# Moving whole rounds of a short convolution from TensorE to VectorE in a fused convolution and multiplicative FFN

## The chip, the cores and the metric

The kernel runs on one core of a Trainium2 chip. The metric is device time in microseconds, and less is better. The time before is the median of 3 runs; a profile shows one further execution.

## The reference

The input `x` has 8 sequences of 3904 tokens with 192 channels. First a causal convolution of 7 taps runs along each sequence. The taps are a softmax over each of 8 heads' weights, and a head has 24 channels. Then a feed-forward network without a nonlinearity other than a product is applied to each token:

```python
# attention-like part: w = softmax(weight, axis=-1), one row of 7 taps for each head of 24 channels
out[b, s, h, g] = sum_k w[h, k] * x_pad[b, s + k, h, g]      # x_pad: 6 zero rows ahead of each sequence
# feed-forward part, on the 31232 tokens
a = x @ w1            # 192 -> 1024
b = x @ w2            # 192 -> 1024
h = a * b @ w3        # (a * b) @ w3, 1024 -> 1024
return h @ w_out      # 1024 -> 192
```

The kernel multiplies `w3 @ w_out` once at its head (`W_sb`, 1024 x 192), so a token needs two first products and one second product.

## The kernel before, in words

The 31232 tokens are two streams of 15616 (`NS = 2`, four sequences each), worked on side by side: stream 0 on partitions 0 to 63 and stream 1 on partitions 64 to 127. The 192 channels are three groups of 64 (`k` = 0, 1, 2). A round `R` is 512 tokens of each stream; there are 31 rounds (`NR`), the last with 256 tokens.

**First product** (`first_product`, L455 to L468): for each of 8 slices of 128 of the hidden width, TensorE multiplies the weights by `xT[k]` (channels on partitions, tokens along the free dimension) into two PSUM tiles `pa` and `pb`. ScalarE copies `pa` to `asb` (L462), VectorE multiplies `asb` by `pb` into `abT` (L464). `xT` is a ring of 4 rounds.

**Second product** (`second_product`, L480 to L488): 32 matmuls of `abT` by `W_sb` for one round and stream, one copy by ScalarE to `osb`, one output DMA on SyncE's queue.

**Convolution on TensorE** (`conv`, L294): tokens are cut into windows of 32 rows that give 26 outputs (`ST`), with the 6 rows ahead. Windows are loaded by GpSimd's DMAs, which cast to bf16, into tiles `xb` (`load_x`, L127), and multiplied by 32x32 band matrices `Aband`, one for each head. The results are evicted to `convo` (L303). Windows are grouped into blocks: `SIZES = [20, 20, 20, 40] + [64] * 7 + [56]`. A *unit* is one call of `conv` for some channels of a block. When all units of a block are done, `store` (L329, L335) writes it to the DRAM array `rows` from SyncE's queue, and `transposes` (L369) brings it back as `xT` by transposing DMAs, also from SyncE's queue. The window in which a new sequence starts needs zero rows ahead of it: GpSimd memsets them in `xb` (L629). From block 4 on (`SPLIT`) the blocks carry two of the three channel groups (`WC = 128`).

**Convolution on VectorE**: the third group, from round 5 on. `cast_c` (L394) casts its channels to a DRAM array `rows_c` from GpSimd's queue, `raw_transpose` (L400) brings two rounds back as `raw`, channels on partitions, and `conv_c` (L410, L414) applies the 7 taps as one multiplication and six multiply-adds with the tap as a scalar of each partition (`wC`), into `xT[2]`. The taps reach `wC` through DRAM (`load_taps`, L377 and L383).

**Order.** The order of instructions on each engine is the order in which the program records them; engines wait for each other by semaphores. After a head, which does rounds 0 to 2, the blocks 0 to 3 and `W_sb`, the loop at L626 goes through phases. Phase p records the first products of rounds 2p+1 and 2p+2 (phase 0 has none), then `conv_c`, then four second products of the rounds 2p and 2p+1, with conv units after the first and, in some phases, after the third (`places`). The transposes are recorded at the end of a phase, and the rounds that they bring are used in the phase after the next:

```python
        if p < len(chunks):
            raw_transpose(p)
        while sent[0] < NR and sent[0] <= LAG + 2 * p + 4 and \
                min((sent[0] + 1) * CH, TS) <= stored[0]:
            transposes(sent[0])
            sent[0] += 1
```

In the head, `load_taps`, `cast_c(0)` and the load of block 5 are recorded in `later_loads`, inside round 0.

Of the kernel before, what the change touches and what calls it, by code (L numbers as in the profile page):

```python
# [11 lines left out]
ALU = mybir.AluOpType  # L12
# [4 lines left out]
def kernel(  # L17
# [29 lines left out]
    WB = -(-S // ST)  # L47
    NWIN = (B // NS) * WB
    LAST = S - (WB - 1) * ST
    LAG_ROWS = (LAG + 1) * CH  # L50
    SIZES = [20, 20, 20, 40] + [64] * 7 + [56]
    SPLIT = 4
    WC = 2 * Q
    assert sum(SIZES) == NWIN
    NB = len(SIZES)
    FIRST = [sum(SIZES[:b]) for b in range(NB)]
    RC = FIRST[SPLIT] * ST // CH
    XN = 32 * WC
    HW = 6

    def tok(i):
        return (i // WB) * S + (i % WB) * ST

# [17 lines left out]
    rows_c = dram.tile([TS, NS * Q], BF16, name="rows_c")  # L81
# [9 lines left out]
    def width_of(b):  # L91
        return D if b < SPLIT else WC

    def parts_of(b):
        return [range(4)] if 4 * shape_of(b)[1] * width_of(b) <= XN else [range(2), range(2, 4)]
# [6 lines left out]
    def runs_of(b, js, e):  # L102
        n, m, E = shape_of(b)
        runs = []
        for s, i in enumerate(FIRST[b] + j * n + u * E + e for j in js for u in range(m)):
            if i < HW or i == NWIN - 1:
                continue
            if runs and tok(i) == runs[-1][1] + runs[-1][2] * E * ST:
                runs[-1][2] += 1
            else:  # L110
                runs.append([s, tok(i), 1])
        return runs

    def load_x(b, parts=(0, 1)):
# [3 lines left out]
        for js in [v for q, v in enumerate(parts_of(b)) if q in parts]:  # L118
            wd = width_of(b)
            xb = work.tile([128, XN], BF16, tag="xb", bufs=6, name="xb")  # L120
            xb = xb[:, 0:len(js) * m * wd].rearrange("p (w d) -> p w d", d=wd)
            for j in js:
                tiles[j] = (xb, (j - js[0]) * m)
            for e in range(E):
                for s, t, w in runs_of(b, js, e):
                    for r in range(NS):
# [3 lines left out]
                                        ap=[[D, C], [E * ST * D, w], [1, wd]]))  # L130
                for j in js:
                    for u in range(m):
                        i, s = FIRST[b] + j * n + u * E + e, tiles[j][1] + u
                        if i % WB == 0 and i:
                            zeros_of += [(xb, group(r, e).start, s) for r in range(NS)]
                        if i == NWIN - 1:
                            nc.gpsimd.memset(xb[group(1, e), s, :], 0.0)
                            t = tok(i) - PAD
                            nc.gpsimd.dma_start(out=xb[group(0, e), s, :],
                                                in_=x_rows[t:t + C, 0:wd])  # L140
                            p = group(1, e).start
                            nc.gpsimd.dma_start(out=xb[p:p + PAD + LAST, s, :],
                                                in_=x_rows[TS + t:TS + t + PAD + LAST, 0:wd])
# [132 lines left out]
    def conv(b, c0, wd, evict=(nc.scalar.copy,), es=None):  # L276
        n, m, E = shape_of(b)
        es = range(E) if es is None else es
        if b not in convo_of:
            convo_of[b] = work.tile([128, n, width_of(b) // Q, NS, Q], BF16, tag="convo", bufs=2,  # L280
                                    name="convo")
            left_of[b] = width_of(b) * E
# [27 lines left out]
    stored, sent = [0], [3]  # L310

    def store(b, first=0):
        stored[0] = tok(FIRST[b] + SIZES[b]) if b + 1 < NB else TS
        n = SIZES[b] // 4
        convo = convo_of[b]
        cols = slice(0, NS * width_of(b))
        for j in range(4):
            w = 0
            while w < n:
                i = FIRST[b] + j * n + w  # L320
                if i < first:
                    w += 1
                    continue
                left = WB - 1 - i % WB
                src = convo[C * j:C * j + ST, w:w + max(1, min(n - w, left))]
                src = src.rearrange("s w k r g -> s w (k r g)")
                j0 = tok(i)
                if left == 0:
                    nc.sync.dma_start(out=rows[j0:j0 + LAST, cols], in_=src[0:LAST, 0, :])  # L329
                    w += 1  # L330
                    continue
                m = min(n - w, left)
                dst = rows[j0:j0 + ST * m, cols].rearrange("(w s) c -> s w c", s=ST)
                for s0, s1 in ((0, 16), (16, ST)):
                    nc.sync.dma_start(out=dst[s0:s1], in_=src[s0:s1])  # L335
# [29 lines left out]
    def transposes(R, first=0):  # L365
        t0, t1 = max(R * CH, first), min((R + 1) * CH, TS)
        a = t0 % RING
        for k in range(NP if R < RC else WC // Q):
# [5 lines left out]
    wC = const.tile([128, K], FP32)  # L374

    def load_taps():
        nc.sync.dma_start(out=taps_d, in_=taps)  # L377
        for r in range(NS):
            c = WC
            while c < D:  # L380
                h = c // G
                c1 = min(h * G + G, D)
                nc.sync.dma_start(out=wC[r * Q + c - WC:r * Q + c1 - WC, :],  # L383
                                  in_=taps_d[h:h + 1, :].to_broadcast([c1 - c, K]))
                c = c1

    chunks = [(R * CH, min((R + 2) * CH, TS)) for R in range(RC, NR, 2)]
    raw_of = {}

    def cast_c(i):  # L390
        t0, t1 = chunks[i]
        t0 = t0 if i else t0 - HALO
        for r in range(NS):
            nc.gpsimd.dma_start(out=rows_c[t0:t1, r * Q:r * Q + Q],  # L394
                                in_=x_rows[r * TS + t0:r * TS + t1, WC:D])

    def raw_transpose(i):
        t0, t1 = chunks[i]
        raw_of[i] = work.tile([128, HALO + 2 * CH], BF16, tag="raw", bufs=2, name="raw")
        nc.sync.dma_start_transpose(out=raw_of[i][:, 0:HALO + t1 - t0],  # L400
                                    in_=rows_c[t0 - HALO:t1, :])

    def conv_c(i):
        t0, t1 = chunks[i]
        raw = raw_of.pop(i)
        acc = work.tile([128, 2 * CH], FP32, tag="acc", bufs=1, name="acc")
        starts = [z for z in range(0, TS, S) if t0 <= z < t1]

        def times(out, lo, hi, d):
            nc.vector.tensor_scalar(out=out, in0=raw[:, HALO + lo - t0 - d:HALO + hi - t0 - d],  # L410
                scalar1=wC[:, K - 1 - d:K - d], scalar2=None, op0=ALU.mult)

        def add(out, lo, hi, d):
            nc.vector.scalar_tensor_tensor(  # L414
                out=out, in0=raw[:, HALO + lo - t0 - d:HALO + hi - t0 - d],
                scalar=wC[:, K - 1 - d:K - d], in1=acc[:, lo - t0:hi - t0],
                op0=ALU.mult, op1=ALU.add)

        times(acc[:, 0:t1 - t0], t0, t1, 1)
        for z in starts:  # L420
            nc.vector.memset(acc[:, z - t0:z - t0 + 1], 0.0)
# [3 lines left out]
        for lo in range(t0, t1, CH):  # L425
            hi = min(lo + CH, t1)
            add(xT[2][:, lo % RING:lo % RING + hi - lo], lo, hi, 0)
# [11 lines left out]
    def first_product(R, between=None):  # L439
# [3 lines left out]
        r0 = (R * CH) % RING  # L443
        per = CH // N if CH % N == 0 else 1
        for f0 in range(0, JT, per):
            pq = []
            for i in range(2):
                p = banks("pa" if i == 0 else "pb")
                pq.append(p)
                for f in range(per):  # L450
                    ft = f0 + f
                    for k in range(NP):
                        for r in range(NS):
# [4 lines left out]
                                xT[k][rs, r0:r0 + N],  # L458
# [15 lines left out]
    def second_product(R, r):  # L474
# [3 lines left out]
        for g in range(ng):  # L478
# [8 lines left out]
        t0 = r * TS + R * CH  # L487
        nc.sync.dma_start(  # L488
            out=out[t0:t0 + ng * 128, :].rearrange("(g p) d -> p g d", p=128), in_=osb)
# [3 lines left out]
    def last_product(R, r):  # L493
        ab = abT_of.pop(R)
        for g, f in zip(range(width(R) // 128), (nc.scalar.copy, nc.vector.tensor_copy) * 2):
# [84 lines left out]
    def later_loads():  # L580
# [6 lines left out]
        load_taps()  # L587
        cast_c(0)
        load_x(5)
# [17 lines left out]
               (store, 3), (transposes, 3), (transposes, 4))})  # L607
    sent[0] = 5
# [4 lines left out]
    units = [(b, c) for b in range(SPLIT, NB) for c in range(0, WC, Q)]  # L613
    loads = [(b, e) for b in range(6, NB) for e in range(len(parts_of(b)))]

    def convolve():
        b, c = units.pop(0)
        conv(b, c, Q, (A, A))
        if c + Q == WC:
            store(b)  # L620

    places = {0: 2, 1: 2, 2: 1, 3: 1, 4: 2, 5: 1, 6: 1, 7: 1, 8: 1, 9: 2, 10: 1, 11: 1}
# [62 lines left out]
```

## Time and profile before

| | |
|---|---|
| median of 3 runs | 520.54 us (519.78 to 521.62) |
| the profiled execution | 517.63 us |
| span in its profile, first to last instruction | 515.9 us |
| TensorE matmuls busy | 510.2 us, 6271 instructions |
| VectorE busy | 423.2 us |
| ScalarE busy | 339.0 us |
| GpSimd busy | 82.9 us |
| first products (L455), all matmuls | 2976 |
| second products (L480) | 1936 matmuls |
| convolution on TensorE (L294) | 1216 matmuls, 222 ns each in the median, many at once |
| convolution on VectorE (L410, L414) | 13 + 106 instructions, 110.7 us |
| DMA, moved | 60.76 MB |

How to read it: PE is TensorE, DVE VectorE, ACT ScalarE, POOL GpSimd and SP SyncE; a `q` behind the name is the engine's queue of instructions that issue DMAs or wait. Matmuls on different parts of TensorE's array overlap, so their durations do not add up to busy time. A timeline row gives start, duration from the first to the last of the instructions that it merges, engine, line, operation, what it writes and reads, and a count. Rows by stretch of time give the stretch, its length, busy microseconds of PE, PEld (weight loads), DVE, ACT and POOL with counts, the granted clock of TensorE, the busy microseconds of a mean DMA engine, and GB/s.

### The profile page before, as it was taken

Reading aid. Unit: us, or ns where it says so; the run is one execution under the profiler, and the core shown is the slowest. Engines: PE = TensorE matmul, PEld = TensorE weight load, DVE = VectorE, ACT = ScalarE, POOL = GpSimd, SP = SyncE. Lnnn points to the kernel's source line nnn. Section 1 sums busy time; section 2 is a strip of 40 time slices with the busy share of each in tenths; the row PEclk is TensorE's granted clock in tenths of the full one; section 3 lists DMA queues with packets and bytes.
Section 4 is the critical chain, followed back from the end, with each engine's and each line's share of the span. In section 5 each row is a group of like instructions: output and inputs, shape, how many; then the busy total and the mean of one; then the engine's idle time right before and its main releaser. Section 6 shows DMA issues by size and latency. Waiting matters only on the chain.

```text
span 515.9 us, 14505 instructions
## 1 busy us (share of the span) xinstructions
PE 510.2 (99%) x6271; PEld 335.7 (65%) x6272; DVE 423.2 (82%) x408; ACT 339.0 (66%) x368; POOL 82.9 (16%) x143
## 2 busy tenths in 40 slices
PE   8999999999999999999999999999999999999997
PEld 4446946748467585674856758567485675856787
DVE  7898189799797997979979799797997979979670
ACT  6886586674765757657576575766757657376562
POOL 9875003041030400404600000000000000000000
PEclk9999999999999999999999999999999999999999
DMA  9999889899498798956990513806525085230304
GB/s 145 147 190 170 143 195 149 163 142 133 116 103 198 97 133 157 123 155 77 168 213 16 155 31 70 176 8 142 110 64 124 1 195 50 69 101 3 123 1 154
DMA packets 164270, 60.76 MB, mean 118 GB/s; under 512 B 113139, under 2 KB 164207, under 8 KB 164207
## 3 DMA queue, kind: packets, MB, share of 16 engines
q1 hardware_dynamic: 92719, 42.65, 36.8%
q0 software_dynamic: 71472, 17.19, 35.8%
q8 instruction: 49, 0.80, 0.6%
q14 instruction: 14, 0.11, 0.1%
q10 hardware_dynamic: 16, 0.00, 0.0%
HBM read 34.66 MB, written 34.82 MB: 135 GB/s over the span
## 4 chain that ended last, share of the span: by engine, by line
PE 97%; DVE 1%; ACT 1%; issue 0%; DVEq 0%
PE ops L480 32%; PE pa L455 30%; PE pb L455 30%; PE cps L294 2%; PE wps L545 1%; PE warm L206 1%; ACT asb L462 1%; DVE abT L464 0%; ACT convo L303 0%; PE ops L498 0%; PE tps L359 0%; PE tps L344 0%; DVE xT L351 0%; DVE xb L248 0%; DVE Aband L258 0%
## 5 line engine op out<-in xcount | busy, mean ns | idle before, releaser
L464 DVE TENSOR_TENSOR abT<-asb,pb 128x1024 bf16<-128x1024 bf16 x240 | 292.9, 1221 | 71.1 <-ACT asb L462 55.3
L462 ACT CAST asb<-pa 128x1024 bf16<-128x1024 f32 x244 | 247.1, 1013 | 63.3 <-PE pa L455 63.0
L455 PE MATMUL pb<-xT,wn 64*128 64x512 bf16 (+1 forms) x744 | 198.3, 373 | 0.0
L455 PE MATMUL pa<-xT,wn 64*128 64x512 bf16 (+1 forms) x744 | 197.5, 373 | 0.2
L455 PE MATMUL pa<-xT,ws 64*128 64x512 bf16 (+1 forms) x744 | 197.5, 373 | 0.0
L455 PE MATMUL pb<-xT,ws 64*128 64x512 bf16 (+1 forms) x744 | 196.2, 373 | 0.1
L455 PEld LDWEIGHTS <-wn 64*128 64x128 bf16 x1488 | 138.1, 94 | 86.0 <-issue 2.2
L455 PEld LDWEIGHTS <-ws 64*128 64x128 bf16 x1488 | 131.5, 94 | 71.0 <-POOL ws L192 0.4
L480 PE MATMUL ops<-W_sb,abT 128*128 128x192 bf16 x1936 | 165.1, 246 | 0.0
L480 PEld LDWEIGHTS <-abT 128*128 128x128 bf16 x1936 | 158.1, 98 | 7.0 <-issue 6.2
L485 ACT COPY osb<-ops 128x768 f32<-128x768 f32 (+1 forms) x61 | 48.5, 795 | 101.2 <-PE ops L480 101.2
L414 DVE SCALAR_TENSOR_TENSOR acc<-raw,wC,acc 128x1024 f32<-128x1024 bf16 (+8 forms) x80 | 83.0, 1066 | 1.9
L303 ACT CAST convo<-cps 128x1024 bf16<-128x1024 f32 (+3 forms) x46 | 37.7, 875 | 1.7 <-PE cps L294 1.6
L127 POOL DMA_DIRECT2D xb<-in_x_dram x54 | 38.1, 713 | 2.9 <-PE pa L455 1.6
L636 POOL COPY pace<-abT 1x2 bf16<-1x2 bf16 x6 | 1.1, 176 | 158.9 <-DVE abT L464 158.9
L394 POOL DMA_DIRECT2D rows_c<-in_x_dram x26 | 20.2, 783 | 2.4 <-DMA xb<-in_x_dram 1.2
L414 DVE SCALAR_TENSOR_TENSOR xT<-raw,wC,acc 128x512 bf16<-128x512 bf16 (+1 forms) x26 | 18.1, 739 | 0.4
L294 PE MATMUL cps<-xb,Aband 32*32 32x192 bf16 (+6 forms) x1216 | 14.5, 225 | 0.5 <-DVE Aband L258 0.5
L294 PEld LDWEIGHTS <-Aband 32*32 32x32 bf16 x1216 | 10.6, 88 | 6.0 <-issue 4.5
L502 DVE COPY osb<-ops 128x192 f32<-128x192 f32 x1 | 0.4, 358 | 11.7 <-PE ops L498 11.7
L410 DVE TENSOR_SCALAR acc<-raw,wC 128x1024 f32<-128x1024 bf16 (+1 forms) x13 | 9.6, 738 | 0.0
L526 POOL DMA_DIRECT2D w3b<-in_moe_w_dram x12 | 7.2, 601 | 2.9 <-DMA xb<-in_x_dram 2.9
(63 smaller groups left out, 74.5 us busy)
## 6 DMA issues: line engine op xcount, KB each, us to landing
out_dram<-osb SPq DMA_DIRECT2D x60, 384.0 KB
xb<-in_x_dram POOLq DMA_DIRECT2D x16, 256.0 KB, 6.7
rows<-convo SPq DMA_DIRECT2D x25, 128.0 KB
rows_c<-in_x_dram POOLq DMA_DIRECT2D x22, 128.0 KB, 6.5
rows<-convo SPq DMA_DIRECT2D x25, 80.0 KB
xb<-in_x_dram POOLq DMA_DIRECT2D x8, 240.0 KB, 6.9
xb<-in_x_dram POOLq DMA_DIRECT2D x6, 216.0 KB, 5.0
w3b<-in_moe_w_dram POOLq DMA_DIRECT2D x4, 256.0 KB, 5.3
```

Of the source, the lines that this page charges most:

```text
L127: nc.gpsimd.dma_start(out=xb[group(r, e), s:s + w, :], in_=bass.AP(tensor=x.tensor, offset=(r * TS + t - PAD) * D, ap=[[D, C], [E * ST * D ...
L294: nc.tensor.matmul(o.rearrange("p (w g) -> p w g", g=wd)[:, :, c - c0:c1 - c0], Aband[group(r, e), h, :], xb[group(r, e), s:s + m, c:c1], ...
L303: f(out=convo[:, e::E, k, :, lo:lo + c] .rearrange("p w r g -> p r w g"), in_=src[:, :, :, o:o + c])
L394: nc.gpsimd.dma_start(out=rows_c[t0:t1, r * Q:r * Q + Q], in_=x_rows[r * TS + t0:r * TS + t1, WC:D])
L410: nc.vector.tensor_scalar(out=out, in0=raw[:, HALO + lo - t0 - d:HALO + hi - t0 - d], scalar1=wC[:, K - 1 - d:K - d], scalar2=None, op0=AL ...
L414: nc.vector.scalar_tensor_tensor(out=out, in0=raw[:, HALO + lo - t0 - d:HALO + hi - t0 - d], scalar=wC[:, K - 1 - d:K - d], in1=acc[:, lo ...
L455: nc.tensor.matmul(p[:, r, f * N:f * N + N], w_of(i, k, r)[rs, ft * 128:(ft + 1) * 128], xT[k][rs, r0:r0 + N], start=(k == 0), stop=(k == ...
L462: nc.scalar.copy(out=asb[:, :, 0:per * N], in_=pa[:, :, 0:per * N])
L464: nc.vector.tensor_tensor(out=ab[:, f0, :, 0:N], in0=asb[:, :, 0:N], in1=pb[:, :, 0:N], op=ALU.mult)
L480: nc.tensor.matmul(ops[:, g // 2, (g % 2) * D:(g % 2) * D + D], ab[:, jt, r, g * 128:(g + 1) * 128], W_sb[:, jt, :], start=(jt == 0), stop ...
L485: nc.scalar.copy(out=osb.rearrange("p (a g) d -> p a (g d)", g=2), in_=ops[:, 0:ng // 2, 0:2 * D])
L526: nc.gpsimd.dma_start(out=t[C * i:C * i + C], in_=bass.AP(tensor=moe_w3.tensor, offset=j0 * 128 * DFF + i * GQ, ap=[[DFF, C], [C * DFF, 4 ...
```

## The change

Instead of one channel group of every round from 5 on, VectorE convolves all three channel groups of two rounds of every third phase: `SIDE = (4, 7, 10, 13)`, that is rounds 9 and 10, 15 and 16, 21 and 22, 27 and 28. The results go to a tile `side`, and `operand` hands it to the first product in place of `xT`. `side_conv` does one channel group of a side phase in each of the three phases ahead of it. TensorE convolves the other rounds with all 192 channels, in blocks of 80 windows (`SIZES = [20, 20, 20, 40, 80, 80, 80, 80, 32]`); a block now covers the rounds between two side phases, and its last window may be cut short or empty. Each phase has one to three units (`places`, now positions among the second products). When a block's last unit is recorded, its store follows, and after the second of the phase's second products the transposes of all its rounds (`due`). `load_taps` now fills taps for all three groups, ends with a copy by GpSimd of one half of `wC` to the other, and is recorded at the end of the head instead of in `later_loads`. The load of block 5 moves from the head to phase 1. Around the last rounds, the output DMA of a second product is split in two and the two engines of the last copies are exchanged.

```diff
+    SIDE = (4, 7, 10, 13)
+    SIZES = [20, 20, 20, 40, 80, 80, 80, 80, 32]
...
+    conv_rounds = [R for R in range(NR) if phase_of(R) not in SIDE]
+    ring_of = {R: i for i, R in enumerate(conv_rounds)}
...
     def load_taps():
         nc.sync.dma_start(out=taps_d, in_=taps)
+        c = 0
+        while c < D:
+            h = c // G
+            c1 = min(h * G + G, (c // Q + 1) * Q)
+            nc.sync.dma_start(out=wC[c % Q:c % Q + c1 - c, c // Q, :],
+                              in_=taps_d[h:h + 1, :].to_broadcast([c1 - c, K]))
+            c = c1
+        P(out=wC[Q:128], in_=wC[0:Q])
...
+    def side_cast(p):
+        t0, t1 = side_span(p)
         for r in range(NS):
+            nc.gpsimd.dma_start(
+                out=rows_c[t0 - HALO:t1, :, r * Q:r * Q + Q],
+                in_=x_rows[r * TS + t0 - HALO:r * TS + t1, :].rearrange("t (k g) -> t k g", g=Q))
+
+    def side_transpose(p, k):
+        t0, t1 = side_span(p)
+        raw_of[p, k] = stage.tile([128, HALO + 2 * CH], BF16, tag="w3T", bufs=2, name="raw")
+        for lo, hi in ((t0 - HALO, t0 + CH), (t0 + CH, t1)):
+            nc.sync.dma_start_transpose(
+                out=raw_of[p, k][:, HALO + lo - t0:HALO + hi - t0], in_=rows_c[lo:hi, k, :])
+
+    def side_conv(p, k):
...
+        nc.vector.tensor_scalar(
+            out=acc, in0=raw[:, HALO - 1:HALO - 1 + t1 - t0], scalar1=wC[:, k, K - 2:K - 1],
+            scalar2=None, op0=ALU.mult)
...
         for d in range(2, K):
             for lo, hi in zip([t0] + [z + d for z in starts], starts + [t1]):
                 add(acc[:, lo - t0:hi - t0], lo, hi, d)
+        add(side_of[p][:, k, :], t0, t1, 0)
+
+    def operand(R, k, rs):
+        if phase_of(R) in SIDE:
+            t0 = R * CH - side_span(phase_of(R))[0]
+            return side_of[phase_of(R)][rs, k, t0:t0 + width(R)]
+        a = ring_of[R] * CH % RING
+        return xT[k][rs, a:a + width(R)]
...
         load_x(4)
         nc.gpsimd.tensor_scalar(out=taps, in0=taps, scalar1=total, scalar2=None, op0=ALU.mult)
-        load_taps()
-        cast_c(0)
-        load_x(5)
+        side_cast(SIDE[0])
...
-               (store, 3), (transposes, 3), (transposes, 4))})
+               (store, 3), (transposes, 3), (transposes, 4), (load_taps,))})
...
+    places = {0: (0, 1, 2), 1: (0,), 2: (0, 2), 3: (0,), 4: (0,), 5: (0, 2), 6: (0,), 7: (0,),
+              8: (0, 2), 9: (0,), 10: (0,), 11: (0,), 12: (0,)}
+    loads = {1: ((5, 0), (5, 1)), 3: ((6, 0), (6, 1)), 6: ((7, 0), (7, 1)), 9: ((8, 0),)}
+    tasks = {q - NP + k: (q, k) for q in SIDE for k in range(NP)}
+    due = []
+
+    def convolve(p):
+        b, h, n = units.pop(0)
+        conv(b, h * G, n * G, (V, A) if p not in tasks else (A, A))
+        if h + n == H:
             store(b)
+            due.extend(block_rounds[b])
...
     for p, rounds in enumerate(phases):
+        for b in {u[0] for u in units[:3]}:
             for xb, p0, w in zero_rows.pop(b, []):
                 nc.gpsimd.memset(xb[p0:p0 + PAD, w, :], 0.0)
+        if p and p + 4 in SIDE:
+            side_cast(p + 4)
         for j, R in enumerate(rounds):
             first_product(R)
+            if j < len(loads.get(p, ())):
                 P(out=pace, in_=abT_of[R][0:1, JT - 1, 1, 0:2])
+                load_x(loads[p][j][0], loads[p][j][1:])
+        if p in tasks:
+            side_conv(*tasks[p])
...
         for n, (R, r) in enumerate(seconds):
             (last_product if (R, r) == (NR - 1, NS - 1) else second_product)(R, r)
+            if n == 1:
+                while due:
+                    transposes(due.pop(0))
+            if n in places.get(p, ()):
+                convolve(p)
+        if p + 1 in tasks:
+            side_transpose(*tasks[p + 1])
```

194 lines of the change are left out of this document (77 added, 117 removed).

## The prediction

> **What bounds the kernel now.** I read the page first: the busy line of TensorE and the chain that ended last.
>
> ```profile
> PE 510.2 (99%) x6271; PEld 335.7 (65%) x6272; DVE 423.2 (82%) x408; ACT 339.0 (66%) x368; POOL 82.9 (16%) x143
> ...
> PE 97%; DVE 1%; ACT 1%; issue 0%; DVEq 0%
> ```
>
> TensorE is busy in 510.2 of 515.9 us and makes up 97% of the chain. No other engine or queue costs time at present. So the change can win only what it takes off TensorE, and it loses every microsecond in which TensorE must wait. I then read TensorE's timeline around one set of second products (phase 3):
>
> ```profile
> 150.21 2.81 PE L480 MATMUL ops<-W_sb,abT 128*128 128x192 bf16 x32
> 152.96 0.68 PE L294 MATMUL cps<-xb,Aband 32*32 32x64 bf16 x64
> 153.57 8.09 PE L480 MATMUL ops<-W_sb,abT 128*128 128x192 bf16 x96
> 161.59 0.39 PE L455 MATMUL pa<-xT,wn 64*128 64x512 bf16 x1
> ```
>
> Call the start of a phase's second products S (here 150.21). The convolution unit stands after the first second product, and the next phase's first products begin at S+11.38. The same stretch without any unit takes 10.67 us (441.23 to 451.90), so this unit of 64 matmuls costs 0.71; the phases with a 48-matmul unit give 0.65. Next, SyncE's queue in the same stretch:
>
> ```profile
> 153.89 0.37 SPq L488 DMA_DIRECT2D out_dram<-osb  x1
> 155.72 5.66 SPq L335 DMA_DIRECT2D rows<-convo  x8
> 161.48 2.68 SPq L488 DMA_DIRECT2D out_dram<-osb  x3
> 164.32 2.39 SPq L400 DMA_TRANSPOSE raw<-rows_c  x1
> 166.81 5.12 SPq L369 DMA_TRANSPOSE xT<-rows  x4
> ```
>
> A block's store starts at S+5.51, after both evictions, and is on the queue for 5.66 us; a transposing load takes 1.28 us each. They fall inside the next phase's first products and serve the phase after it: a lead of a whole phase, 32 us. When they land is seen in the DMA share, one row per microsecond:
>
> ```profile
> 171.00:172.00 1.00, 1.00 (x14) 0.49 (x10) 0.93 (x2) 0.72 (x2) 0.00 (x0) 1.00 0.51 110
> 172.00:173.00 1.00, 1.00 (x12) 0.52 (x10) 0.93 (x2) 0.72 (x2) 0.00 (x0) 1.00 0.64 148
> 173.00:174.00 1.00, 1.00 (x12) 0.54 (x10) 0.87 (x2) 0.83 (x1) 0.08 (x1) 1.00 0.00 0
> ```
>
> The share falls to zero at 173.0, and the last transpose was issued at 170.7: it lands about 2.2 us after its issue begins. Last, SyncE and GpSimd at the end of the head, where load_taps is moved:
>
> ```profile
> 44.06 2.49 SPq L383 DMA_DIRECT2D wC<-taps_d  x6
> 46.67 7.91 SPq L335 DMA_DIRECT2D rows<-convo  x10
> 55.34 8.34 SPq L369 DMA_TRANSPOSE xT<-rows  x6
> ```
>
> ```profile
> 45.33 0.45 POOL L629 MEMSET xb<- 6x128 bf16 x2
> 45.72 1.53 POOL L394 DMA_DIRECT2D rows_c<-in_x_dram  x2
> ```
>
> Block 4's zero rows are written at 45.33, and TensorE reads that block at 54.99. That is 9 us of cover.
>
> **The change, part by part.** *Convolution on TensorE.* Before: 8 units at 0.65 and 8 at 0.71, 10.9 us. After: 16 units of 32 matmuls of 240 columns (blocks of 80) and 2 of 64 (the block of 32). Of a unit's 0.71, 0.61 is matmuls and 0.10 the change of form. If instructions decide, 32 cost 32 x 9.5 ns = 0.31, with the 0.10 it is 0.41; if columns decide, 7680 against 8192 of the 0.56 unit, 0.63. I take 0.50: 16 x 0.50 + 2 x 0.71 = 9.4, a gain of **1.5 us** (bounds: a loss of 0.5, a gain of 2.9).
>
> *VectorE.* Thirteen chunks become twelve side_convs, each 0.75 + 6 x 1.285 = 8.5 us by the rows of L410 and L414; a sequence start inside adds about 1.1. They start at S+1.64 as now (119.70 against 118.06) and end by S+11.3; VectorE is next wanted once the next pair of products is done, past S+12.4, and side rounds read the third channel group at S+11.6. Cost nothing; without that cover at most 1 us in each of a few phases. ScalarE's evictions shrink from 1024 to 960 columns. The split output DMAs and the swapped engines of the last product: within 0.3 us.
>
> *Late transposes.* This is the first wait that is added. Block 4 has its last unit in phase 1, block 5 in phase 4, block 6 in phase 7, block 7 in phase 10, each after the first second product; the store follows, and the transposes of the block's four rounds follow the second one. The next phase begins with the first of these rounds. The lead of a phase is gone. Step by step from S: store begins at S+5.4; it has 9 to 12 DMAs and 2048 row pieces of 768 B instead of 1664 of 512 B. The 3 output DMAs above (1536 pieces of 768 B in 2.68) would make that 3.6 us, the bytes against the store's 5.66 would make it 10.4; I take 6, nearest to the store's own row by count. Then one output DMA, 0.6: S+12.0. Third transpose begins 2.6 later and lands 2.2 after that: S+16.8. TensorE wants it 0.43 after its first products could begin at S+11.2, so at S+11.6: it waits **5.2 us**, with the bounds of the store 2.9 and 9.7. Even with no throttling at all the queue needs 9 x 0.35 + 0.4 + 2.6 + 2.2 after S+5.4, so 2 us of wait remain. In phases 4, 7 and 10: 3 x 5.2 = **15.7**.
>
> In phase 1 the store meets other traffic: the second half of block 5's load is issued by GpSimd right after round 4's products, and the side cast for phase 7 stands right behind it in GpSimd's queue, with nothing to wait for (some 2560 and 6240 row pieces). In the profile the stretch 76 to 92 us has the same mix: a load and cast issued from 77.18, transposes issued from 77.01, and the DMA share stays at 0.81 to 0.93 to the end at 92, against 8.7 us for the same transposes alone (164.32 to 173.0). So contention may add 0 to 9 us; I take 6: **11.2 us** in phase 1.
>
> *Zero rows behind the taps.* load_taps now ends with a GpSimd copy of wC, and stands in SyncE's queue behind the transposes of rounds 3 and 4. In the changed kernel's order on GpSimd the copy comes first, then the two memsets of block 4's zero rows; the ninth matmul of the first unit of phase 0 waits for them. Queued behind the copy are the memsets, behind them TensorE. Its time: transposes off SyncE's queue at 63.7 now (55.34 + 8.34), one store DMA more, 64.0; taps_d issued, 0.4; its landing 2.2 (the transpose's row; 4.1 is what SyncE waited for it in the busy head); ten wC loads at 0.415 (2.49 for 6), 4.2; landing of the last 2; copy and memset 0.4: 73.2. TensorE arrives at 55.1 (54.99 now). It waits **18.1 us**, between 16 and 21. The side cast in this place, with block 5's load gone, keeps the DMAs busy to about 54 as now, so the stores are not later.
>
> *TensorE's clock after such waits.* The page grants 1.0 throughout, and has no long wait once running. What it has is the start:
>
> ```profile
> 1.27 2.74 PE L206 MATMUL warm<-zeros 128*128 128x512 bf16 x6 [1.27 <-DVE zeros L150]
> ```
>
> Six matmuls of 512 columns in 2.74 us are 0.45 each, where a pair of 512 columns later takes 0.215: half speed from 1.27 to about 5 us, some 2 us lost. I charge 2 us for each of the two long waits, **4 us**; bounds 0 and 10 (all five). [...]
>
> Sum: -1.5 + 15.7 + 11.2 + 18.1 + 4 = **+47.5 us**. The profiled execution took 517.63 (span 515.9), so 565.1 for one like it; the median of the runs lies 2.9 higher, 520.54, and gives 568.
>
> **Rivals.** (a) *Not slower: the waits are covered and only the cheaper units show.* Place: the ninth matmul of phase 0 and the third transpose of phases 1, 4, 7, 10. It decides if the zero rows are written by 55.1 and the transposes land by S+11.6. For it: DMA engines are half idle after 90 us. Against: the queue's own issue times already exceed both limits. Price -1.5: 519.0. (b) *The clock drops at all five waits.* For: each wait is 3 us or more without any matmul. Against: in the short ones the first two channel groups come 1.3 us apart and wake it. 6 more: 574. (c) *The zero rows hold nothing up* (TensorE's wait is met earlier than the queue order says): the late transposes alone, 47.5 - 18.1 - 2: 548. Against: order and waits name that memset. (d) *The transposes come in time, the zero rows don't*: 18.1 + 2 - 1.5: 539.
>
> **How the numbers follow.** Forecast as summed 0.58, (a) 0.04, (b) 0.20, (c) 0.11, (d) 0.07. The predicted time is the forecast's, 568. Its own bounds (waits of 2.9 to 9.7 three times, 5 to 14 in phase 1, 16 to 21 in phase 0, clock 0 to 10) do not all fall together; 552 to 582 covers them, and down to 547 takes in (c). Left out are (a), (d) and the tails. About 0.3% (1.6 us) is what a measurement of this kernel can tell from no change; (a) lies just at it, so it is shared between faster and same: 0.02 and 0.02, slower 0.96.
>
> **What would show it.** In the changed kernel: a TensorE gap of about 18 us near 55, released by a GpSimd memset; gaps of about 5 us at the head of phases 5, 8 and 11 and a longer one at phase 2, released by DMA transposes of xT; SyncE showing twelve transposes in a row some 12 us after S; cps groups of 32 matmuls in about 0.4 us; matmuls of twice the length right after the gaps if the clock drops. A TensorE busy share still at 99% would make the prediction wrong altogether; a gap at 55 but none at phase 5 would make it (d).

## The result: 15% slower, and the profile after

The changed kernel takes **597.24 us** (median of 5 runs, 596.01 to 601.5) against 519.78 us before (median of 5 runs in the same comparison). The ratio is 1.1495, with a 95% interval of 1.1456 to 1.1534. The prediction was 568 us with a range of 547 to 582: the direction held, the size did not.

The profiled execution is the longest of the five, 601.5 us; its span is 599.3 us, 83.4 us more than the 515.9 us of before. The page of the changed kernel, first the busy times, then two rows of forty slices (TensorE's busy share and its granted clock, in tenths), then the chain that ended last:

```profile
PE 524.3 (87%) x6015; PEld 339.5 (57%) x6016; DVE 419.4 (70%) x411; ACT 339.2 (57%) x387; POOL 75.1 (13%) x130
...
PE   8998099908999997599999929999995799999997
...
PEclk8999589957999999699999968999998799999999
...
PE 78%; SPq 10%; DMA 7%; ACT 2%; issue 1%; DVE 1%; POOL 0%; POOLq 0%; ACTq 0%
```

TensorE's share in the chain falls from 97% to 78%, and 17% now belongs to SyncE's queue and to DMAs. The busy row has five holes, and the clock row has a dip at each of them. The list of waits names who ends them (total, number of waits, longest, in us):

```profile
PE pa L470 <- DMA xT<-rows: 51.2, 10, 17.4
...
POOL wC L393 <- DMA wC<-taps_d: 23.4, 1, 23.4
...
PE cps L305 <- POOL xb L650: 17.3, 1, 17.3
```

**Hole 1, in phase 0.** TensorE's timeline and GpSimd's:

```profile
54.46 2.81 PE L495 MATMUL ops<-W_sb,abT 128*128 128x192 bf16 x32
57.20 0.29 PE L305 MATMUL cps<-xb,Aband 32*32 32x240 bf16 x8
74.79 0.90 PE L305 MATMUL cps<-xb,Aband 32*32 32x240 bf16 x24 [17.30 <-POOL xb L650]
```

```profile
74.24 0.20 POOL L393 COPY wC<-wC 64x21 f32<-64x21 f32 x1 [23.36 <-DMA wC<-taps_d]
74.49 0.55 POOL L650 MEMSET xb<- 6x192 bf16 x2
...
110.25 3.73 POOL L146 DMA_DIRECT2D xb<-in_x_dram  x6
113.98 2.65 POOL L403 DMA_DIRECT2D rows_c<-in_x_dram  x2
```

TensorE stops after eight convolution matmuls, at the ninth, as the prediction said. GpSimd's copy of `wC` waited 23.4 us for the taps' DMAs, the two memsets of zero rows stood behind it, and TensorE behind them. When it goes on, 24 matmuls take 0.90 us and the next second product 5.27 us (75.63 to 80.90) instead of 2.81: half clock. The last two rows are the end of block 5's load and the side cast behind it, which share the DMAs with block 4's store in phase 1.

**Holes 3, 4 and 5, after phases 4, 7 and 10.** TensorE around the end of phase 4 (S = 224.44), and SyncE's queue in the same stretch:

```profile
227.54 8.10 PE L495 MATMUL ops<-W_sb,abT 128*128 128x192 bf16 x96
245.84 0.60 PE L470 MATMUL pa<-xT,wn 64*128 64x512 bf16 x1 [10.20 <-DMA xT<-rows]
```

```profile
228.12 0.37 SPq L505 DMA_DIRECT2D out_dram<-osb  x1
229.84 10.49 SPq L343 DMA_DIRECT2D rows<-convo  x8
240.38 0.87 SPq L336 DMA_DIRECT2D rows<-convo  x1
241.35 1.36 SPq L505 DMA_DIRECT2D out_dram<-osb  x1
242.80 15.60 SPq L377 DMA_TRANSPOSE xT<-rows  x12
```

The store is on the queue from 229.84 to 241.25, 11.4 us, where before's took 5.66. One output DMA and then twelve transposes follow. The second channel group comes 1.0 us after the first and the third another 1.2 us later, so 12.0 us are lost to waiting here, 12.4 after phase 7 and 12.0 after phase 10. Hole 2, after phase 1, is 17.4 us.

In rows by stretch of time (columns as before, the DMA figure being a share of the stretch), the end of the hole after phase 4:

```profile
240.00:245.00 5.00, 0.00 (x0) 0.00 (x0) 0.00 (x0) 0.00 (x0) 0.00 (x0) 0.50 0.71 170
245.00:250.00 5.00, 3.18 (x14) 1.06 (x16) 0.00 (x0) 1.01 (x1) 0.00 (x0) 0.50 0.50 112
```

The clock is 0.50 in the wait and remains there when the work resumes. A pair of first products takes 20.83 us undisturbed; after the five holes the loss beyond the waiting is 3.1, 2.8, 1.6, 2.8 and 1.9 us. The records of the granted clock show what it is. The clock returns to 1.00 at 80.74, 142.18, 251.40, 364.04 and 473.27, which is 6.0, 5.8, 3.4, 5.7 and 3.8 us after the work has resumed in full, and half of each of these times is the loss, within 0.15 us.

| us | predicted | in the profile |
|---|---|---|
| convolution units, 10.9 before | -1.5 | -2.1 (16 at 0.46, 2 at 0.73) |
| zero rows behind the taps, phase 0 | 18.1 | 17.4 |
| late transposes after phase 1 | 11.2 | 17.4 |
| late transposes after phases 4, 7, 10 | 15.7 | 36.4 |
| half clock after the waits | 4 | 12.2 |
| sum | 47.5 | 81.3 |
| this execution's head: S of phase 0 at 54.46, 52.24 before | | 2.2 |

The sum and the head make 83.5 us; the span grew by 83.4. The head's 2.2 us do not come from the change: in this execution the granted clock is 0.50 from 9.06 to 12.47 us. Of the fourteen profiles of this document three have such a stretch in the head, with S of phase 0 at 54.46 to 54.81; in the other eleven, before's among them, it lies at 52.09 to 52.49.

### The profile page after: what moved, and what is told of

The parts are those of the page before. It is cut to its first block, busy times and chain, and to the rows that moved or that the text cites. A ratio compares the mean times of both kernels' runs of the same rounds, so it can differ in the third digit from the quotient of the medians.

```text
span 599.3 us, 13971 instructions
## 1 busy us (share of the span) xinstructions
PE 524.3 (87%) x6015; PEld 339.5 (57%) x6016; DVE 419.4 (70%) x411; ACT 339.2 (57%) x387; POOL 75.1 (13%) x130
## 3 DMA queue, kind: packets, MB, share of 16 engines
q0 software_dynamic: 60416, 17.44, 28.6%
## 4 chain that ended last, share of the span: by engine, by line
PE 78%; SPq 10%; DMA 7%; ACT 2%; issue 1%; DVE 1%; POOL 0%; POOLq 0%; ACTq 0%
PE pa L470 27%; PE pb L470 26%; PE ops L495 22%; SPq L343 6%; DMA rows<-convo 3%; DMA xT<-rows 3%; SPq L377 2%; ACT convo L314 1%; PE cps L305 1%; PE wps L563 1%; DMA xb<-in_x_dram 1%; SPq L505 1%; SPq L390 0%; SPq L336 0%; ACT asb L477 0%
## 5 line engine op out<-in xcount | busy, mean ns | idle before, releaser
L470 PE MATMUL pa<-xT,wn 64*128 64x512 bf16 (+1 forms) x552 | 153.5, 385 | 50.6 <-DMA xT<-rows 50.2
L470 PE MATMUL pa<-xT,ws 64*128 64x512 bf16 (+1 forms) x552 | 153.6, 386 | 1.0 <-DMA xT<-rows 1.0
L470 PE MATMUL pb<-xT,wn 64*128 64x512 bf16 (+1 forms) x552 | 151.9, 382 | 0.0
L470 PE MATMUL pb<-xT,ws 64*128 64x512 bf16 (+1 forms) x552 | 149.5, 382 | 0.0
L428 DVE SCALAR_TENSOR_TENSOR acc<-raw,wC,acc 128x1024 f32<-128x1024 bf16 (+10 forms) x90 | 78.7, 925 | 1.3
L470 PE MATMUL pb<-side,wn 64*128 64x512 bf16 x192 | 51.9, 376 | 0.0
L470 PE MATMUL pa<-side,wn 64*128 64x512 bf16 x192 | 51.7, 376 | 0.0
L470 PE MATMUL pa<-side,ws 64*128 64x512 bf16 x192 | 51.7, 376 | 0.0
L470 PE MATMUL pb<-side,ws 64*128 64x512 bf16 x192 | 51.4, 376 | 0.0
L314 ACT CAST convo<-cps 128x640 bf16<-128x640 f32 (+4 forms) x65 | 38.0, 659 | 20.3 <-PE cps L305 20.2
L305 PEld LDWEIGHTS <-Aband 32*32 32x32 bf16 x960 | 7.1, 88 | 24.4 <-issue 23.7
```

Of the source, the lines that this page charges most:

```text
L305: nc.tensor.matmul(o.rearrange("p (w g) -> p w g", g=wd)[:, :, c - c0:c1 - c0], Aband[group(r, e), h, :], xb[group(r, e), s:s + m, c:c1], ...
L314: f(out=convo[:, e::E, k, :, lo:lo + c] .rearrange("p w r g -> p r w g"), in_=src[:, :, :, o:o + c])
L428: nc.vector.scalar_tensor_tensor(out=out, in0=raw[:, HALO + lo - t0 - d:HALO + hi - t0 - d], scalar=wC[:, k, K - 1 - d:K - d], in1=acc[:, ...
L470: nc.tensor.matmul(p[:, r, f * N:f * N + N], w_of(i, k, r)[rs, ft * 128:(ft + 1) * 128], operand(R, k, rs), start=(k == 0), stop=(k == NP ...
```

## The experiments

Theory A is the prediction's mechanism: five waits, one from the order on GpSimd, four from stores and transposes with no phase of lead. The rivals were that a wait taken away only uncovers another, that VectorE's longer work is a second bound, and, for the sizes, what sets the store's duration.

### Zero rows ahead of the copy

```diff
     def load_taps():
...
-        P(out=wC[Q:128], in_=wC[0:Q])
...
         for b in {u[0] for u in units[:3]}:
             for xb, p0, w in zero_rows.pop(b, []):
                 nc.gpsimd.memset(xb[p0:p0 + PAD, w, :], 0.0)
+        if p == 0:
+            P(out=wC[Q:128], in_=wC[0:Q])
```

> The changed kernel with one edit: GpSimd's copy of wC is recorded behind the two memsets of block 4's zero rows instead of ahead of them. Theory A (TensorE's first long wait is GpSimd's queue order: the memsets stand behind a copy that waits for the tap loads): the wait of 17.4 us at the first unit of phase 0 and the half clock behind it (2.4 us) go, 597 becomes about 577; the waits at the head of phases 2, 5, 8 and 11 stay (17.4, 12.0, 12.4, 12.0 us in the profile). Rival B (the wait is for block 4's own load, which is late): the gap stays within 1 us of 17.4.

Measured: 576.27 us, 21.0 less than the changed kernel. Its GpSimd timeline:

```profile
50.40 0.55 POOL L649 MEMSET xb<- 6x192 bf16 x2
74.64 0.20 POOL L651 COPY wC<-wC 64x21 f32<-64x21 f32 x1 [23.68 <-DMA wC<-taps_d]
```

The memsets are done at 51.0, the copy still waits its 23.7 us, and now nobody waits for it: TensorE's hole in phase 0 is gone with its half clock (17.4 + 3.1 = 20.5 by the table). The other four stay: 16.4 us to the first channel group after phase 1, and 10.5, 11.0 and 10.5 after phases 4, 7 and 10. So the waits add up, as Theory A has it, and this one is the order on one queue.

### A phase of lead given back

The fourth unit of each block goes into the phase before its own, and all transposes are recorded at the end of the phase. The second kernel is this with the zero rows ahead of the copy.

```diff
-    places = {0: (0, 1, 2), 1: (0,), 2: (0, 2), 3: (0,), 4: (0,), 5: (0, 2), 6: (0,), 7: (0,),
-              8: (0, 2), 9: (0,), 10: (0,), 11: (0,), 12: (0,)}
+    places = {0: (0, 1, 2, 3), 2: (0, 2), 3: (0, 2), 5: (0, 2), 6: (0, 2),
+              8: (0, 2), 9: (0, 2), 11: (0,), 12: (0,)}
...
-            if n == 1:
-                while due:
-                    transposes(due.pop(0))
...
         if p + 1 in tasks:
             side_transpose(*tasks[p + 1])
+        while due:
+            transposes(due.pop(0))
```

> The changed kernel with the fourth unit of each block of 80 one phase earlier, and the block's transposes recorded at the end of that phase, so that they have a phase of lead again; the copy of wC stays where it is. Theory A (four waits come from the lost lead, not from the store being slow as such): the four waits of together 53.8 us and the half clock behind them (9.1 us) go; the first wait stays at about 17.4; about 597 - 63 = 534. Rival C (the queue itself is too full: 9 to 12 store DMAs and 12 transposes of 1.3 us each do not fit): later work on SyncE's queue is late instead, the side transposes or the output DMAs, and more than 15 us of waits remain, 550 or more.

> Both edits, rows first and the lead. If the prediction's terms were the whole of it, only the gain in convolution units is left (10.9 us before, 8.8 in the changed kernel's profile): 519.8 - 2.1 = 517.7, faster than the kernel before by 0.2 to 0.6%. If VectorE's or SyncE's new work has a cost of its own that the waits have hidden, 521 or more.

Measured: 568.91 and 559.52 us, 35 more than expected for the first. The edit had a flaw: at the end of phase 0 the transposes of rounds 7 and 8 go to the ring places of rounds 3 and 4, which phase 1 has yet to use. So rounds 3 and 4 are computed from other rounds' data, and TensorE waits at the head of phase 1 until all twelve transposes have landed. The second kernel's waits:

```profile
PE pa L469 <- DMA xT<-rows: 40.3, 3, 38.9
```

All the same, the waits after phases 4, 7 and 10 are gone in both: the first products begin 0.18 us after the start of the last matmul of the second products, as everywhere in the kernel before. The lead was what those three lacked. The mended edit lets transposes through only two rounds past what the next phase uses:

```diff
-        while due:
+        while due and due[0] <= 2 * p + 6:
             transposes(due.pop(0))
```

> Rows first and the lead, as in e3_both, but at the end of a phase only the transposes of rounds up to 2p+6 are recorded, so that rounds 7 and 8 don't overwrite the ring places of rounds 3 and 4. Theory A (the two orders are the whole loss): no wait over 1 us is left behind the head, and only the gain in convolution units shows: 519.6 - 2.1 = 517.5, ratio 0.994 to 0.998. Rival C (SyncE's queue or VectorE's side work costs something of its own): 521 or more.

Measured: 528.23 us (ratio to before 1.0165, 1.0134 to 1.0195), 10.7 over what was expected. Two waits had been behind the ones removed:

```profile
DVE acc L420 <- DMA raw<-rows_c: 14.1, 1, 14.1
```

VectorE's first `side_conv` waits 14.1 us for `raw`, because its transposing load now stands behind block 4's store in SyncE's queue; and TensorE waits 7 us for `xT` at the head of phase 2. The rest of the kernel runs without a hole.

### What the store costs

Two kernels change the store of the blocks from 4 on. The first stores two of three channel groups, so pieces of 512 B instead of 768 B, in the same DMAs. The second keeps the bytes and issues them in DMAs of at most ten windows, the four groups of partitions in turn.

```diff
+        cw = NP * 128 if b < 4 else 256
...
-                    src = convo[C * j:C * j + ST, w:w + m].rearrange("s w k r g -> s w (k r g)")
-                    dst = rows[t:t + ST * m, :].rearrange("(w s) c -> s w c", s=ST)
+                    src = convo[C * j:C * j + ST, w:w + m].rearrange("s w k r g -> s w (k r g)")[:, :, 0:cw]
+                    dst = rows[t:t + ST * m, 0:cw].rearrange("(w s) c -> s w c", s=ST)
```

> The changed kernel, storing only two of the three channel groups of blocks 4 to 8 (row pieces of 512 B instead of 768 B, the same number of pieces and DMAs); the third group of these rounds is read from the second's columns, so its part of the output is not computed. The store took 11.4 us in phase 4 of the changed kernel (9 DMAs, 2048 pieces, 1.57 MB). Theory D (the store is limited by bytes, near 140 GB/s, as the kernel before with 0.85 MB in 5.66 us): 1.05 MB take 7.4 us, and the waits of 12.0 to 12.4 us shrink by 4 us each. Rival E (limited by the number of pieces, 180 in a us): 11.4 us as before, waits as before.

```diff
-                    for s0, s1 in ((0, 16), (16, ST)):
-                        nc.sync.dma_start(out=dst[s0:s1], in_=src[s0:s1])
+                    for g in range(0, m, 10 if b >= 4 else m):
+                        mg = min(10 if b >= 4 else m, m - g)
+                        src = convo[C * j:C * j + ST, w + g:w + g + mg].rearrange("s w k r g -> s w (k r g)")
+                        dst = rows[t + ST * g:t + ST * (g + mg), :].rearrange("(w s) c -> s w c", s=ST)
+                        parts[min(g // 10, 1)] += [(dst[s0:s1], src[s0:s1]) for s0, s1 in ((0, 16), (16, ST))]
                 w += m
+        for dst, src in parts[0] + parts[1]:
+            nc.sync.dma_start(out=dst, in_=src)
```

> The changed kernel with the stores of blocks 4 to 8 cut into DMAs of at most 10 windows, the first 10 windows of all four partition groups ahead of the second 10 (16 to 19 DMAs instead of 9 to 12, the same bytes and pieces). Theory F (the store is slow because the DMAs in flight read the same 26 partitions, 20 pieces each): it goes toward the 300 pieces in a us that block 3's store reached in the head, 7 to 8 us instead of 11.4, and the waits at the head of phases 5, 8 and 11 shrink from 12.0-12.4 to 8 or 9. Theory D (a store is limited by bytes alone, near 140 GB/s): 11 us or more, waits of 12 or more.

Measured, SyncE's queue in phase 4 of the first and then of the second:

```profile
225.69 7.80 SPq L344 DMA_DIRECT2D rows<-convo  x8
233.53 0.67 SPq L337 DMA_DIRECT2D rows<-convo  x1
```

```profile
224.27 0.32 SPq L337 DMA_DIRECT2D rows<-convo  x1
225.13 9.78 SPq L348 DMA_DIRECT2D rows<-convo  x16
```

With two thirds of the bytes in as many pieces the store takes 8.5 us instead of 11.4, and the three waits are 7.6 us each instead of 12.0 to 12.4 (584.79 us in its one run, 12 less). So it is not the number of pieces, by which it would have stayed at 11.4. By bytes alone it would have been 7.6, which is near; a line through both points has 2.7 us to begin with and 5.5 us for each MB. The second kernel, with 16 DMAs instead of 8 and the four groups of partitions in turn, took 10.6 us from the first row's start to the end of the last; its first DMA also began 0.9 us sooner after S, and the waits became about 10.0 us (591.62 us, one run). So the partitions in flight are worth at most 0.8 of the 11.4 us in this form; most of the store's duration remains.

What sets the byte rate is left open. On the queue the store takes 11.4 us for 1.57 MB, 138 GB/s; before's store 5.66 us for 0.85 MB, 150 GB/s; and three outputs, from 128 partitions, 2.68 us for 1.18 MB, which the prediction took as its lower bound. But the transfer goes on behind the row of the queue. By the DMA packets in the trace of before, its store's pieces begin from 156.56 to 164.27, over 7.7 us, where the row ends at 161.38, and those of the three outputs from 162.69 to 167.48, over 4.8 us, where the row ends at 164.16. A piece of 768 B keeps a DMA engine busy for 39 ns as part of these outputs, and for 71 ns in the mean as part of the changed kernel's store (231 to 240 us). Two stretches of the changed kernel, one with block 3's store in the head and one with block 5's in phase 4:

```profile
56.00:57.50 1.50, 1.50 (x24) 1.16 (x22) 0.18 (x1) 0.19 (x1) 0.00 (x0) 1.00 1.31 291
231.00:240.00 9.00, 4.64 (x57) 4.41 (x54) 3.85 (x5) 1.79 (x3) 0.00 (x0) 0.88 0.76 132
```

One of this store's DMAs reads 16 or 10 partitions, and the kernel with all groups in turn gained only 0.8 of the 11.4 us. But block 3's store in the head, whose DMAs read 16 or 10 partitions too, moved 489 of its pieces from 56.0 to 57.5 us, at 39 ns each: 250 GB/s of the 291, where the second row has 132. So the number of partitions alone does not explain the rate, and no run here shows what does.

### The side cast out of the way in phase 1

```diff
-        if p and p + 4 in SIDE:
-            side_cast(p + 4)
...
+            if p and p + 5 in SIDE and j == 0:
+                P(out=pace, in_=abT_of[R][0:1, JT - 1, 1, 0:2])
+                side_cast(p + 5)
```

> The changed kernel with the side cast for phase 7 held back to phase 2 by a pace copy (those for phases 10 and 13 to phases 5 and 8), so that it is off the DMA engines while phase 1's store and transposes run. Theory H (the wait at the head of phase 2 is longer than the other three because this cast and block 5's load share the DMA engines): it shrinks from 17.4 us toward 13 to 14 (block 5's load stays). Rival I (block 4's store is longer by its own 12 DMAs): it stays at 17. The other waits stay.

Measured: 594.29 us (one run). TensorE at the head of phase 2:

```profile
128.67 0.61 PE L470 MATMUL pa<-xT,wn 64*128 64x512 bf16 x1 [11.59 <-DMA xT<-rows]
...
130.74 0.58 PE L470 MATMUL pa<-xT,wn 64*128 64x512 bf16 x1 [0.76 <-DMA xT<-rows]
```

The wait after phase 1 is 13.3 us (11.7 to the first channel group, the rest to the next two) instead of 17.4; after phases 4, 7 and 10 it is 10.6 to the first channel group, as with the cast in place (10.3 to 10.5). The same wait with the cast in place was 16.4 in the kernel with the zero rows ahead of the copy. So the cast cost 3 to 4 of the 17.4, and only in phase 1: the contention is real, and it is not the whole of that wait.

### Keeping TensorE busy through the wait

Forty-six matmuls of zeros, 128x512, are issued at the end of phases 4, 7 and 10; their results are not used.

```diff
         if p + 1 in tasks:
             side_transpose(*tasks[p + 1])
+        if p in (4, 7, 10):
+            warm(46)
```

> The changed kernel with 46 dummy matmuls of 128x512 on zeros (9.9 us at full clock) recorded behind the second products of phases 4, 7 and 10, inside waits of 12.0 to 12.4 us. Theory J (what is lost behind a wait is TensorE's clock, halved while it stood still): the waits for xT land at the same times, and first products behind them take 20.5 us as elsewhere instead of 21.7 to 22.9; the granted clock stays 1.0 there, 1.6 to 2.8 us are won in each of the three phases. Rival K (the loss is ScalarE or VectorE catching up): the first products stay as long as they were.

Measured: 596.03 us (one run). The transposes land when they did, and the stretch that was empty above now reads

```profile
240.00:245.00 5.00, 4.97 (x24) 2.06 (x21) 0.00 (x0) 0.00 (x0) 0.00 (x0) 1.00 0.67 163
```

with the clock at 1.00. After phases 4 and 10 the loss beyond the waiting is 0.0 us instead of 1.6 and 1.9; after phase 7 it is 1.7 instead of 2.8, since the clock fell for one stretch of 3.41 us (356.52 to 359.94) just when the last channel group came, at 356.27. So the loss after these waits is the clock's. The 4.4 us that these three phases win are read from the trace: the time of the one run lies within the changed kernel's own 596.01 to 601.5.

### Taking away what was behind

Starting from the mended lead, the taps are scaled and loaded ahead of the side cast and the first `raw` transposes are recorded in the head, ahead of block 4's store; the second kernel also holds the later side casts back by a phase.

```diff
+        nc.gpsimd.tensor_scalar(out=taps, in0=taps, scalar1=total, scalar2=None, op0=ALU.mult)
+        load_taps()
...
-               (store, 3), (transposes, 3), (transposes, 4), (load_taps,))})
+               (store, 3), (transposes, 3), (transposes, 4), (side_transpose, SIDE[0], 0))})
...
-        if p + 1 in tasks:
+        if p and p + 1 in tasks:
             side_transpose(*tasks[p + 1])
```

> e7_lead_two with two more orders on SyncE's queue: the taps are scaled and loaded at the start of later_loads (no longer between round 4's transposes and block 4's store), and the first side transpose is recorded in the head, ahead of block 4's store instead of behind it. In e7's profile VectorE waited 14.1 us for that transpose in phase 1 and TensorE for xT at the head of phase 2; the two phases took 11.5 us more than the same work later. Theory A (all that is left in e7 is SyncE's queue in phases 0 and 1): these 11.5 us go, 528.2 becomes 516.7 to 518, faster than the kernel before by 0.2 to 0.6%. Rival L (DMA traffic in phases 0 and 1, not the order, is what is late): 523 or more.

> e9_taps_raw_early with the side casts held back by a pace copy as in e5_cast_later. If DMA traffic in phase 1 still costs something in e9, this is faster than e9 by that; if the order was the whole, it is within 0.2% of e9.

Measured: 523.76 us (ratio 1.0071, 1.0035 to 1.0107) and 524.19 us (1.007, 1.0044 to 1.0096). VectorE's wait is gone. TensorE still meets holes at the head of phase 2: there the first products begin 1.8 us late and then stop for each channel group of round 5, which lands only between 98 and 102 us. Holding the casts back changed nothing, so the cast is not what delays round 5; what is left in that stretch beside its store and transposes is block 5's load. Two kernels moved it: all of it behind round 6's transposes, or its second half behind round 5's (this is the second's edit).

```diff
-                P(out=pace, in_=abT_of[R][0:1, JT - 1, 1, 0:2])
+                if (p, j) == (1, 1):
+                    a = ring_of[5] * CH % RING
+                    P(out=pace, in_=xT[2][0:1, a:a + 2])
+                else:
+                    P(out=pace, in_=abT_of[R][0:1, JT - 1, 1, 0:2])
                 load_x(loads[p][j][0], loads[p][j][1:])
```

> e9_taps_raw_early with both halves of block 5's load (and so the side cast for phase 7 behind them in GpSimd's queue) held back by a pace copy that reads round 6's xT, so that they start when the transposes of rounds 5 and 6 have landed. In e9's profile two phases still took 7.8 us more than the same work later, with xT of round 5 landing at 98 to 102 us. Theory M (DMA traffic of phase 1: block 4's store and these transposes share the engines with block 5's load): the 7.8 us go, 523.8 becomes 516 to 518, ratio to before 0.993 to 0.997. Rival N (the store from 73 us on is late by itself): within 2 us of e9.

> e9_taps_raw_early with only the second half of block 5's load (and the side cast for phase 7 behind it) held back, by a pace copy that reads round 5's xT; the first half stays behind round 3 as in e9. In e11 the wait for xT at the head of phase 2 was gone, but the load came so late that phase 2's first unit waited 4.7 us for it; block 4's store took 13.6 us there against 14.8 with the first half's load beside it. Theory M: no wait over 1 us is left behind the head, and only the cheaper units show, 516 to 518.5, ratio to before 0.993 to 0.998. Rival: one of the two waits comes back by 2 us or more, 520 or more.

Measured: the whole load behind, 520.92 us (1.0018, 0.9994 to 1.0043). The wait for `xT` is gone, and the load is now too late instead: the second products of phase 2 with their two units take 16.3 us up to the next first products, where they take 11.6 elsewhere. Half the load behind: **515.89 us** (515.73 to 516.06 in 6 runs) against 519.85 before, a ratio of 0.9916 (0.9887 to 0.9945). Its page:

```profile
PE 508.8 (99%) x6016; PEld 333.6 (65%) x6016; DVE 420.2 (82%) x412; ACT 338.1 (66%) x386; POOL 74.7 (15%) x130
...
PE 96%; ACT 1%; DVE 1%; DMA 1%; issue 0%; POOL 0%; ACTq 0%; POOLq 0%
```

TensorE is back at 99% with VectorE's convolution as in the changed kernel. Every full pair of first products after phase 1 takes 20.83 us, and no first product waits for `xT`. The span is 514.0, 1.9 less than before's 515.9, near the 2.1 that the units gain. The medians differ by 4.0; the kernel before spreads from 518.6 to 523.5 us in that comparison while its profiled execution took 517.63. Four of its eleven executions there have a granted clock of 0.997 and take 521.26 to 523.51 us, which fits one half-clock stretch like that in the changed kernel's head; the six of this kernel have 0.999 or 1.000. What the other seven, 518.62 to 519.86 us, lose against the profiled execution, no trace shows.

## Why the prediction was right and wrong

**Right: the five places, their releasers and their order.** TensorE stops at the ninth matmul of phase 0's first unit, released by a memset, for 17.4 us (18.1 predicted; 16.3 to 18.8 in the other profiles with this order), and the kernel with the memsets ahead of the copy takes that away. At the heads of phases 2, 5, 8 and 11 it waits for `xT`; with a phase of lead the last three are gone.

**Right: the cover on VectorE.** No wait of TensorE for `side` or for `abT` came in, and the kernel without holes runs 12 side convolutions at no cost. The 14.1 us that VectorE waited in one experiment were for a DMA, not for its own work.

**Right in sign, a little small: the units.** 32 matmuls of 240 columns cost 0.46 with the change of form (0.50 taken): 2.1 won instead of 1.5.

**Wrong: the store, the term that carries most of the miss.** The step was "I take 6, nearest to the store's own row by count", between 3.6 by the outputs' rate and 10.4 by bytes. It begins at S+5.40, as predicted, and takes 11.4, beyond even the upper bound. Of the 6.8 us by which the waits after phases 4 and 10 are longer (7.2 after phase 7), 5.4 are the store; the output DMA behind it is about 1 later than taken (1.36 on the queue, behind a store still in flight) and the landing 0.4. The choice of the row was the error. Before's own store has the same sources and the same kind of rows, and by bytes it gives 10.4; the outputs have other sources, and the count of pieces does not set the time, as the experiment with 512-B pieces shows. With 10.4 the three waits would have been summed at 9.7 each, the upper bound that the prediction gave, 29 us instead of 15.7. The bound itself was low because 5.66 us is the row of the queue: the pieces of before's store take 7.7, and by bytes that makes 14.2, above the 11.4 measured.

**Wrong for the same reason: the wait after phase 1.** The contention was put at 6 on top of the wait of 5.2. It is 5.0 to 5.4 by the difference to the other three, of which the cast accounts for 3 to 4. So that term was near, and the missing 6.2 us are the store's again: on the queue it takes 12.7 us there (113.26 to 125.98) where 6 were taken.

**Wrong: the clock.** The forecast charged two long waits with 2 us each; the rival that all five drop was the true one, and it was given 0.20. The reason against it was that the channel groups come 1.3 us apart and wake the clock. They do come so (1.0 and 1.2), but the few matmuls of one group did not bring the clock back: after phase 4 it is 0.50 from 237.75, inside the wait, to 251.40, 3.4 us after the third group came at 248.04. The price was low too, 12.2 over five drops instead of 10. It is not the bursts that made it higher: the two waits that ended at a stroke lost 3.1 and 2.8. In the records of the granted clock the half-speed stretches of the changed kernel last 3.41 us or a multiple of it, up to 20.5. The clock fell 2.1 to 2.8 us after the last matmul had ended in four of the five waits, and 4.8 us after it in the one behind phase 7. A drop cost 1.6 to 3.1 us, where the forecast took 2 from the half speed at the start of the kernel before.

So the forecast of 568 fell 29 us short of the median. In the profile, whose execution is 4.3 us above the median, the terms fell short by 33.8: 20.7 from the three late transposes, 6.2 from phase 1, 8.2 from the clock, less 0.6 in the units and 0.7 in phase 0. The range did not reach it because its bounds for the store ended at 10.4 and the terms were taken as if they could not all fall on one side; but three waits and a half of the fourth hang on one store rate, so they fall together.

## What to carry to other kernels

Price a transfer that moves onto the path by the row that has its own sources and its own bytes, however different its count, and read its length by its pieces, since its row on the queue can end before they are moved. Where several terms of a sum hang on one such price, let the range move them together. When an instruction that waits for a DMA is recorded on a queue, read what stands behind it there: a copy of 0.2 us cost 20 us because two memsets followed it. A store and its twelve transposes, 28.6 us on the queue here, need a phase of lead; with that lead, and no load that competes with the first of them, the change itself is worth about 2 us of TensorE's time (514.0 against 515.9 us in the profiles; the medians differ by 0.8%).

## What the runs showed of the hardware that was not expected

A store that reads 16 or 10 partitions at a time went through the queue at 138 to 150 GB/s in the phases and reached 250 GB/s for a stretch in the head, and splitting it into 16 DMAs over all partitions shortened it by 7% only. The clock of TensorE did not come back for single channel groups: in the wait after phase 4 it was 0.50 although work arrived 1.0 and 1.2 us apart, and 46 idle matmuls in the wait kept it at 1.00. And the same transfer can have a price in one order and none in another: holding back the side casts took 3 to 4 us off the wait after phase 1 in the changed kernel, and nothing (523.76 against 524.19 us) in the kernel where block 5's load delayed round 5.
